# Sigmoid attention with a token mixer: one batch per partition half, row and column tiles throughout, whole-row q and k loads on one queue

## The chip, the cores and the metric

The kernel runs on one core of one Trainium2 chip (trn2). The metric is the time of one execution on the device in microseconds (us), inputs and outputs in the chip's main memory. Each kernel was run several times; each run carries a state, fast or slow, and only fast runs are compared. A profile is one execution; its span is 1.5 to 2.5 us shorter than the time of the same run.

In the profile lines PE is TensorE, PEld its weight loads, DVE VectorE, ACT ScalarE, POOL GpSimd; SPq and ACTq are the instruction queues of SyncE and ScalarE. A timeline line gives start and duration in us, engine, line of kernel.py, operation, output <- inputs, for TensorE the tile of the array (rows*columns) and the shape, and how many of them; in brackets stands how long the engine was idle before, and what ended that. On TensorE the outputs are ptq, ptk, px and pk (transposes of q, k, x and wk), sc (scores), pv (values), pw (wq/wk), pt (tmp = wk.T @ x), pm (mix) and po (output). The granted clock is the share of TensorE's full clock that it got in a stretch.

## The reference

```python
batch, n_heads, seq, head_dim = 8, 12, 448, 64
S = 448; scale = 1 / sqrt(64)
scores = scale * q @ k.T - log(S)
attn   = 1 / (1 + exp(-scores))             # sigmoid, no row sum
x      = (attn @ v)                          # 8 x 12 x 448 x 64 -> 8 x 448 x 768
# the token mixer, weights w_q, w_k (768 x 64), w_out (768 x 768)
wq, wk = x @ w_q, x @ w_k                    # 448 x 64 per batch
mixed  = (scale * wq @ wk.T) @ x             # the kernel computes wq @ (wk.T @ x)
out    = maximum(mixed, 0) @ w_out           # fp32, 8 x 448 x 768
```

Everything comes and goes in fp32: 11 MB each of q, k, v and output. On the chip it is cast to bf16. There is a sigmoid for each of 8 x 12 x 448 x 448 scores, and those are ScalarE's work.

## The kernel before

Work is cut into 4 units of two batches, and each unit into 6 pairs of heads. A pair is: loads, casts (GpSimd), transposes of q and k (TensorE, copied out by VectorE), 14 score matmuls, 7 sigmoids on two of them at a time (ScalarE), two bursts of values matmuls. The mixer of unit u-1 is dealt out among the scores of unit u by a list of estimated costs.

The loads alternate between two queues; `nc.scalar` is ScalarE's own instruction stream:

```python
queues = (nc.sync, nc.scalar)
def load_qk(u, j):
    for nm, src in (("q", q), ("k", k)):
        t = p_ld.tile([P, 2, NI * HD], F32, tag=nm + "32", name=nm + "32")
        for b2 in range(2):                              # 64 partitions each
            queues[b2].dma_start(out=t[64 * b2 : 64 * b2 + 64], in_=...)
# load_v: 4 transfers of 64 partitions, two on each queue; load_vr: 4 more per unit, in 256-byte pieces
```

Scores use the whole 128 x 128 array with zeros: the two heads of a pair lie on the two partition halves and kz holds each head's keys with zeros on the other half.

```python
for gg in range(NI):                                     # 7 groups of 2 score blocks
    sc = ps_s.tile([P, 2, 512], F32, ...)                # two buffers
    for slot in range(2):
        nc.tensor.matmul(sc[:, slot, 0:S], kzt[u, j][:, b2, m * P : (m + 1) * P], qt[u, j][:, b2, :], ...)
    nc.scalar.activation(at, sc[:, :, 0:S], ACTF.Sigmoid, bias=bias_t, scale=attn_scale)
    ...                                                  # values burst, then pieces of the mixer
```

Of the kernel before, what the change touches and what calls it, by code (L numbers as in the profile page):

```python
# [12 lines left out]
ALU = mybir.AluOpType  # L13

PV_COL = True
# [3 lines left out]
def kernel(  # L19
# [14 lines left out]

    nc = tc.nc
# [10 lines left out]
    KPOS = [2 * i if i < 4 else 2 * (i - 4) + 1 for i in range(NI)]  # L46
# [10 lines left out]
    p_vr = pool("vr", 2)  # L57
    p_w32 = pool("w32", 3)
    p_c16 = pool("c16", 2)
    p_qt = pool("qt", 2)  # L60
    p_at = pool("at", 10)
    p_x = pool("x", 2)
# [3 lines left out]
    ps_v = pool("ps_v", 1, space=bass.MemoryType.PSUM)  # L66
    ps_f = pool("ps_f", 3, space=bass.MemoryType.PSUM)


    NKZ = 3  # L70
    kz = [singles.tile([P, 2, NI * P], BF16, name=f"kz{n}") for n in range(NKZ)]
    if PV_COL:
        v16 = [[singles.tile([P, NJ, 2, 3, HD], BF16, name=f"v16{n}{b}") for b in range(2)] for n in range(2)]
        vr16 = [[singles.tile([P, NJ, P], BF16, name=f"vr16{n}{b}") for b in range(2)] for n in range(2)]
        vzero = [t for n in range(2) for t in vr16[n]]
    else:
        vz = [[singles.tile([P, NJ, NI, P], BF16, name=f"vz{n}{b}") for b in range(2)] for n in range(2)]
        vzero = [t for n in range(2) for t in vz[n]]
    wqbd = singles.tile([P, NI, 2, NP], BF16, name="wqbd")
    wkts = singles.tile([P, NI, 2, NP], BF16, name="wkts")  # L80
    wout16 = singles.tile([P, NC, D], BF16, name="wout16")
    wqk = [singles.tile([P, NC, P], BF16, name=f"wqk{b}") for b in range(2)]
    wq32 = singles.tile([P, NC, DH], F32, name="wq32")
    wk32 = singles.tile([P, NC, DH], F32, name="wk32")
    ident = singles.tile([P, P], F32)
    bias_t = singles.tile([P, 1], F32)
    ident16 = singles.tile([P, P], BF16)

    ctx.enter_context(tc.manual_schedule())


    queues = (nc.sync, nc.scalar)
    ld = {}

    def load_qk(u, j):
        for nm, src in (("q", q), ("k", k)):
            t = p_ld.tile([P, 2, NI * HD], F32, tag=nm + "32", name=nm + "32")
            for b2 in range(2):
                queues[b2].dma_start(  # L99
                    out=t[64 * b2 : 64 * b2 + 64],  # L100
                    in_=src[2 * u + b2, 2 * j : 2 * j + 2].rearrange("h (p i) d -> p h (i d)", i=NI),
                )
            ld[nm, u, j] = t

    def load_v(u, j):
        for b2 in range(2):
            t = p_ld.tile([P, 2, 3 * HD], F32, tag=f"v32{b2}", name="v32")
            base = v[2 * u + b2, 2 * j]

            for par, (off, step) in enumerate(((0, S + 4), (4, S - 3))):  # L110
                queues[par].dma_start(  # L111
                    out=t[64 * par : 64 * par + 64],
                    in_=bass.AP(
                        base.tensor, base.offset + off * HD,
                        [[NI * HD, NP], [step * HD, 2], [1, 3 * HD]],
                    ),
                )
            ld["v", u, j, b2] = t

    def load_vr(u):  # L120
        for b2 in range(2):
            t = p_vr.tile([P, NJ, HD], F32, tag=f"vr32{b2}", name="vr32")
            for hh, i in ((0, 3), (1, 0)):
                queues[hh].dma_start(
                    out=t[64 * hh : 64 * hh + 64],
                    in_=v[2 * u + b2].rearrange("(j h) (p i) d -> h i p j d", h=2, i=NI)[hh, i],
                )
            ld["vr", u, b2] = t


    def cast_qk(u, j, eng_q=nc.gpsimd):
        for nm, eng in (("q", eng_q), ("k", nc.gpsimd)):
            t16 = p_c16.tile([P, NI, 2, HD], BF16, tag=nm + "16", name=nm + "16")
            eng.tensor_copy(  # L134
                out=t16.rearrange("p i h d -> p h i d"),
                in_=ld.pop((nm, u, j)).rearrange("p h (i d) -> p h i d", i=NI),
            )
            ld[nm + "16", u, j] = t16

    def cast_v(u, j):  # L140
        for b2 in range(2):
            t = ld.pop(("v", u, j, b2))
            if PV_COL:
                nc.gpsimd.tensor_copy(  # L144
                    out=v16[u % 2][b2][:, j].rearrange("p h m d -> p (h m d)"),
                    in_=t.rearrange("p h x -> p (h x)"),
                )
            else:
                z = vz[u % 2][b2]
                for hh in range(2):  # L150
                    nc.gpsimd.tensor_copy(
                        out=z[:, j, 4 * hh : 4 * hh + 3, 64 * hh : 64 * hh + 64],
                        in_=t[:, hh].rearrange("p (m d) -> p m d", m=3),
                    )

    def cast_vr(u):
        for b2 in range(2):
            t = ld.pop(("vr", u, b2))
            for hh in range(2):
                r = slice(64 * hh, 64 * hh + 64)  # L160
                dst = vr16[u % 2][b2][r, :, r] if PV_COL else vz[u % 2][b2][r, :, 3, r]
                nc.gpsimd.tensor_copy(out=dst, in_=t[r])


    qt, kzt = {}, {}
    nkz = [0]

    def tr_q(u, j):
        st = {}

        def f(i):
            if i == 0:
                st["p"] = ps_f.tile([P, 2, NI, NP], BF16, tag="f", name="ptq")
            nc.tensor.transpose(  # L174
                st["p"][:, :, i, :], ld["q16", u, j][:, i].rearrange("p h d -> p (h d)"), ident16
            )
            if i == NI - 1:
                t = p_qt.tile([P, 2, NI * NP], BF16, tag="qt", name="qt")
                nc.vector.tensor_copy(out=t, in_=st["p"].rearrange("p b i n -> p b (i n)"))  # L179
                qt[u, j] = t  # L180
        return [(60, lambda i=i: f(i)) for i in range(NI)]

    def tr_k(u, j):
        st = {}

        def f(i):
            if i == 0:
                st["p"] = ps_f.tile([P, 2, NI, NP], BF16, tag="f", name="ptk")
            nc.tensor.transpose(  # L189
                st["p"][:, :, KPOS[i], :], ld["k16", u, j][:, i].rearrange("p h d -> p (h d)"), ident16  # L190
            )
            if i == NI - 1:
                z = kz[nkz[0] % NKZ]
                nkz[0] += 1
                for hh in range(2):
                    r = slice(64 * hh, 64 * hh + 64)
                    nc.vector.tensor_copy(  # L197
                        out=z[r, :, S * hh : S * hh + S],
                        in_=st["p"][r].rearrange("p b i n -> p b (i n)"),
                    )  # L200
                kzt[u, j] = z
        return [(60, lambda i=i: f(i)) for i in range(NI)]
# [4 lines left out]
    def mlp(u):  # L207
        xt = xts[u]
        st = {}

        def wqk_mm(b2, c):
            if c == 0:
                st["w", b2] = ps_f.tile([P, NI, NP], F32, tag="f", name="pw")
            nc.tensor.matmul(  # L214
                st["w", b2], wqk[b2][:, c, :], xt[c][:, :, b2, :],
                start=(c == 0), stop=(c == NC - 1),
            )
            if c == NC - 1:
                rq = slice(64 * b2, 64 * b2 + 64)
                rk = slice(64 - 64 * b2, 128 - 64 * b2)  # L220
                nc.vector.tensor_copy(out=wkts[rk, :, b2, :], in_=st["w", b2][rk])
                nc.vector.tensor_copy(out=wqbd[rq, :, b2, :], in_=st["w", b2][rq])  # L222

        def x_tr(i, c):
            if i == 0 and c == 0:
                st["xn"] = p_one.tile([P, NI, D], BF16, tag="xn", name="xn")
            if c == 0:
                st["px"] = ps_f.tile([P, D], BF16, tag="f", name="px")
            nc.tensor.transpose(  # L229
                st["px"][:, c * P : (c + 1) * P],  # L230
                xt[c][:, i].rearrange("p b n -> p (b n)"), ident16,
            )
            if c == NC - 1:
                nc.vector.tensor_copy(out=st["xn"][:, i, :], in_=st["px"])

        def wk_tr(i):
            if i == 0:
                st["pk"] = ps_f.tile([P, NI, 2, 64], BF16, tag="f", name="pk")
            nc.tensor.transpose(
                st["pk"][:, i].rearrange("p b n -> p (b n)"),  # L240
                wkts[:, i].rearrange("p b n -> p (b n)"), ident16,
            )
            if i == NI - 1:
                st["wkn"] = p_one.tile([P, NI, 2, 64], BF16, tag="wkn", name="wkn")
                for b2 in range(2):
# [245 lines left out]
```

## Time and profile before

| | before |
|---|---|
| time, median of 4 | 314.8 us (311.94 to 419.04; the 419 is a single slow run) |
| first sigmoid | 17.5 us |
| first unit, no mixer in it | 64.5 us |
| units 2, 3, 4 | 68, 69, 61 us |
| tail, from about the last sigmoid | 32.2 us |
| load rate from 2 to 42 us | 247 GB/s |

A unit is read from one wq/wk stage to the next. The first unit, which has neither mixer nor output in it, is hardly shorter than the others. No engine is full there.

### The profile page before, as it was taken

The numbers are of one execution on the slowest core, as the hardware profiler recorded it, in microseconds if no ns is written. First come the engines' busy times: TensorE is split into PE (matmuls) and PEld (weight loads), VectorE is DVE, ScalarE is ACT, GpSimd is POOL, SyncE is SP. The second block draws the span as 40 slices with busy tenths as digits, with TensorE's granted clock in tenths as the row PEclk, the third lists the DMA queues.
The fourth block names the chain that finished last, engine by engine and source line by source line (L and its number), as shares of the span: only waits on it lengthen the run. The fifth ranks groups of instructions, "written<-read, shape, count | busy, mean of one in ns | idle before, by whom it ended". The sixth has DMA issues, their size and how long they took to land.

```text
span 312.2 us, 4870 instructions
## 1 busy us (share of the span) xinstructions
PE 249.2 (80%) x1740; PEld 132.8 (43%) x1740; DVE 155.0 (50%) x271; ACT 175.6 (56%) x193; POOL 80.8 (26%) x128
## 2 busy tenths in 40 slices
PE   1476675777889889499869889599869889998994
PEld 0223222333445445255446445255445445545452
DVE  3522322333566746245646646245656646548662
ACT  0086375487656766467745766448745768770210
POOL 1640832553312302333032312323032303000000
PEclk9999859877999999799998999699999999999998
DMA  8999998656430365947990375948991265232076
GB/s 176 247 235 288 216 257 190 157 117 163 96 86 0 86 186 136 218 122 200 246 224 5 82 185 143 214 110 212 240 227 27 63 187 134 53 101 52 0 178 176
DMA packets 40984, 47.11 MB, mean 151 GB/s; under 512 B 12032, under 2 KB 36608, under 8 KB 40960
## 3 DMA queue, kind: packets, MB, share of 16 engines
q1 hardware_dynamic: 23936, 30.29, 39.8%
q10 hardware_dynamic: 17024, 16.52, 22.2%
q8 instruction: 13, 0.21, 0.3%
q14 instruction: 11, 0.09, 0.1%
HBM read 35.78 MB, written 11.01 MB: 150 GB/s over the span
## 4 chain that ended last, share of the span: by engine, by line
PE 50%; DMA 22%; ACTq 8%; ACT 6%; DVE 6%; issue 3%; POOL 2%; SPq 1%; POOLq 0%
PE sc L439 16%; PE po L281 15%; DMA q<-in_q_dram 10%; PE pv L368 8%; ACT at L446 6%; DMA k<-in_k_dram 5%; ACTq L99 4%; ACTq L111 3%; DMA vr<-in_v_dram 3%; PE pt L253 3%; DMA v<-in_v_dram 3%; PE ptk L189 2%; PE pm L265 2%; PE pw L214 2%; DVE kz L197 2%
## 5 line engine op out<-in xcount | busy, mean ns | idle before, releaser
L446 ACT ACTIVATE at<-sc,bias_t 128x896 bf16<-128x896 f32 x168 | 164.2, 1007 | 91.3 <-PE sc L439 38.2
L439 PE MATMUL sc<-qt,kz 128*128 128x448 bf16 x336 | 99.4, 383 | 41.2 <-ACT at L446 40.2
L281 PE MATMUL po<-wout,mx 128*128 128x384 bf16 x336 | 67.2, 335 | 0.0
L439 PEld LDWEIGHTS <-kz 128*128 128x128 bf16 x336 | 30.8, 102 | 74.4 <-issue 63.2
L134 POOL CAST q<-q 128x896 bf16<-128x896 f32 x23 | 21.5, 933 | 158.0 <-DMA q<-in_q_dram 113.5
L377 DVE CAST xt<-pv 128x448 bf16<-128x448 f32 x48 | 30.0, 625 | 48.5 <-PE pv L368 48.5
L287 DVE COPY o<-po 128x384 f32<-128x384 f32 x56 | 31.2, 558 | 36.2 <-PE po L281 35.7
L281 PEld LDWEIGHTS <-mx 128*128 128x128 bf16 x336 | 33.4, 100 | 26.0 <-issue 3.7
L197 DVE COPY kz<-ptk 64x896 bf16<-64x896 bf16 x48 | 29.8, 621 | 23.4 <-PE ptk L189 23.0
L368 PE MATMUL pv<-at,v 128*64 128x448 bf16 x288 | 39.1, 381 | 0.0
L179 DVE COPY qt<-ptq 128x896 bf16<-128x896 bf16 x24 | 15.0, 624 | 24.2 <-PE ptq L174 23.9
L134 POOL CAST k<-k 128x896 bf16<-128x896 f32 x24 | 22.4, 933 | 15.3 <-DMA k<-in_k_dram 10.2
L144 POOL CAST v<-v 128x384 bf16<-128x384 f32 x48 | 23.1, 506 | 5.9 <-DMA v<-in_v_dram 3.9
L368 PEld LDWEIGHTS <-v 128*64 128x64 bf16 x288 | 12.7, 113 | 24.3 <-issue 21.1
L272 ACT ACTIVATE mx<-pm 128x448 bf16<-128x448 f32 x24 | 13.0, 541 | 17.3 <-PE pm L265 17.3
L174 PE MATMUL ptq<-ident,q 128*128 128x128 bf16 x168 | 15.3, 228 | 9.2 <-DVE q L134 5.8
L189 PE MATMUL ptk<-ident,k 128*128 128x128 bf16 x168 | 19.3, 246 | 1.6 <-POOL k L134 1.6
L265 PE MATMUL pm<-wqbd,tmp 128*128 128x448 bf16 x48 | 15.6, 353 | 4.7 <-DVE kz L197 2.9
L174 PEld LDWEIGHTS <-q 128*128 128x128 bf16 x168 | 12.1, 102 | 14.9 <-DVE q L134 5.8
L189 PEld LDWEIGHTS <-k 128*128 128x128 bf16 x168 | 14.1, 111 | 9.2 <-issue 4.4
L368 PE MATMUL pv<-at,vr 128*64 128x448 bf16 x96 | 17.7, 362 | 0.0
L229 PE MATMUL px<-ident,xt 128*128 128x128 bf16 x168 | 14.5, 231 | 1.6 <-DVE wqbd L222 0.7
(35 smaller groups left out, 126.7 us busy)
## 6 DMA issues: line engine op xcount, KB each, us to landing
out_dram<-o SPq DMA_DIRECT2D x56, 192.0 KB, 2.7
q<-in_q_dram ACTq DMA_DIRECT2D x24, 224.0 KB, 3.6
q<-in_q_dram SPq DMA_DIRECT2D x24, 224.0 KB, 4.9
k<-in_k_dram ACTq DMA_DIRECT2D x24, 224.0 KB, 4.2
k<-in_k_dram SPq DMA_DIRECT2D x24, 224.0 KB, 5.5
v<-in_v_dram ACTq DMA_DIRECT2D x48, 96.0 KB, 4.7
v<-in_v_dram SPq DMA_DIRECT2D x48, 96.0 KB, 4.8
w<-in_moe_w_out_dram SPq DMA_DIRECT2D x6, 384.0 KB, 5.9
```

The lines of the kernel that those rows point to most:

```text
L134: eng.tensor_copy(out=t16.rearrange("p i h d -> p h i d"), in_=ld.pop((nm, u, j)).rearrange("p h (i d) -> p h i d", i=NI),)
L144: nc.gpsimd.tensor_copy(out=v16[u % 2][b2][:, j].rearrange("p h m d -> p (h m d)"), in_=t.rearrange("p h x -> p (h x)"),)
L174: nc.tensor.transpose(st["p"][:, :, i, :], ld["q16", u, j][:, i].rearrange("p h d -> p (h d)"), ident16)
L189: nc.tensor.transpose(st["p"][:, :, KPOS[i], :], ld["k16", u, j][:, i].rearrange("p h d -> p (h d)"), ident16)
L197: nc.vector.tensor_copy(out=z[r, :, S * hh : S * hh + S], in_=st["p"][r].rearrange("p b i n -> p b (i n)"),)
L265: nc.tensor.matmul(pm, st["tmp"][:, c * P : (c + 1) * P], wqbd.rearrange("p i b n -> p (i b n)")[:, hf * S : (hf + 1) * S], start=True, st ...
L281: nc.tensor.matmul(st["po"], st["mx"][c][:, i * P : (i + 1) * P], wout16[:, c, nb * NB : (nb + 1) * NB], start=(c == 0), stop=(c == NC - 1),)
L287: nc.vector.tensor_copy(out=st["o"][:, nb * NB : (nb + 1) * NB], in_=st["po"])
L368: nc.tensor.matmul(ps[c], w, ats[u, j, b2, 4 * hh + m if m < 3 else 3], start=(m == 0), stop=(m == 3),)
L377: nc.vector.tensor_copy(out=xts[u][j][:, :, b2, :], in_=ps)
L439: nc.tensor.matmul(sc[:, slot, 0:S], kzt[u, j][:, b2, m * P : (m + 1) * P], qt[u, j][:, b2, :], start=True, stop=True,)
L446: nc.scalar.activation(at, sc[:, :, 0:S], ACTF.Sigmoid, bias=bias_t, scale=attn_scale)
```

## The change

The intent: the two batches of a unit take the two partition halves. The transposes of a pair then write two column tiles (64 output rows each), the scores of a head are two row tiles (contraction 64 each, no zeros), and so on through the mixer. The loads of q and k become whole: 128 partitions (two heads x 64) per transfer, on SyncE's queue (one k at the start excepted); v stays in four transfers of 64 partitions. The mixer's parts come in blocks at fixed places. A one-element sigmoid at the start also brings ScalarE's table load forward: it took 1.28 us directly ahead of the first sigmoid before.

```diff
-    queues = (nc.sync, nc.scalar)
...
+    def load1(n, nm, eng):
+        t = p_ld.tile([P, 2, NI * HD], F32, ...)
+        eng.dma_start(out=t, in_=dict(q=q, k=k)[nm][2*u : 2*u+2, 2*j : 2*j+2].rearrange(
+            "b h (p i) d -> (h p) b (i d)", i=NI))
...
+    def scores(n, g):                       # 6 of these, plus one for the leftover keys in column tiles
+        h, m = divmod(g, 3)
+        for b2 in range(2):                 # HALF = partitions 0..63, 64..127
+            nc.tensor.matmul(sc[:, b2, 0:S], kts[n][HALF[b2], h, m*P : (m+1)*P], qts[n][HALF[b2], h, :], ...)
+        sigmoid(n, g, sc)
...
     for n, (u, j) in enumerate(pairs):
+        if n + 3 < N:                       # q, k three pairs ahead (were two)
+            load1(n + 3, "q", nc.sync)
+            load1(n + 3, "k", nc.sync)
+        if n + 2 < N:
+            load_v(n + 2, nc.sync)
...
+        if n + 1 < N: tr_q(n + 1)           # 14 column-tile transposes (were 7 whole ones)
+        scores_last(n)
+        if n + 1 < N: tr_k(n + 1)           # 16
+        if n >= 2: tr_x(n - 2)              # 16
+        if u > 0 and j == 1: mlp_wkn(u - 1)
+        scores(n, 0); scores(n, 1)
+        whole(left)                         # up to two output groups of 6 matmuls
+        scores(n, 2); scores(n, 3)
+        if n > 0: values(n - 1, 0); values(n - 1, 1)
+        if u > 0 and j == 1: mlp_tmp(u - 1)
+        scores(n, 4); scores(n, 5)
+        if u > 0 and j == 0: mlp_wqk(u - 1)
+        elif u > 0 and j == 1:
+            for c in range(NC): mlp_mix(u - 1, c)
+            outs += outs_of(u - 1)
+        else: whole(left - 1)
```

(The one-line `if` forms are shortened here.)

## The prediction

> **What bounds the kernel now.** I read the busy shares and the chain of the page first, then the stages by windows (cut at the first sigmoid, just ahead of the wq/wk matmuls of each unit of two batches, and at the last values matmuls), then who waits for whom on ScalarE, then two stretches of the timeline.
>
> ```profile
> PE 249.2 (80%) x1740; PEld 132.8 (43%) x1740; DVE 155.0 (50%) x271; ACT 175.6 (56%) x193; POOL 80.8 (26%) x128
> ...
> PE 50%; DMA 22%; ACTq 8%; ACT 6%; DVE 6%; issue 3%; POOL 2%; SPq 1%; POOLq 0%
> ...
> L446 ACT ACTIVATE at<-sc,bias_t 128x896 bf16<-128x896 f32 x168 | 164.2, 1007 | 91.3 <-PE sc L439 38.2
> ```
>
> TensorE is busiest, but it has only half of the chain; 30% of the chain are transfers and the issuing of transfers on ScalarE's queue. The stages say where:
>
> ```profile
> 0.00:17.50 17.50, 5.09 (x31) 3.16 (x32) 7.99 (x15) 1.30 (x2) 7.34 (x18) 1.00 0.90 216
> 17.50:82.00 64.50, 46.00 (x264) 20.67 (x264) 18.71 (x30) 40.88 (x43) 25.17 (x38) 0.84 0.82 197
> 82.00:150.00 68.00, 58.27 (x435) 31.74 (x435) 36.72 (x64) 43.35 (x49) 18.57 (x28) 0.97 0.52 129
> 150.00:219.00 69.00, 58.93 (x423) 32.80 (x423) 36.98 (x65) 43.11 (x48) 18.67 (x28) 0.93 0.65 155
> 219.00:280.00 61.00, 54.96 (x412) 29.48 (x409) 34.92 (x61) 43.27 (x48) 11.08 (x16) 1.00 0.55 132
> 280.00:312.20 32.20, 26.00 (x180) 15.01 (x179) 19.66 (x37) 3.69 (x7) 0.00 (x0) 0.96 0.39 98
> ```
>
> Columns: stretch, length, busy us of PE, PEld, DVE, ACT, POOL, then granted clock, DMA share, GB/s. A start of 17.5 us without a sigmoid; a first unit with nothing of the mixer in it that is almost as long (64.5) as the units with it (68, 69, 61); a tail of 32.2. The first unit is not bound by an engine: it holds 46.0 us of PE and 40.9 of ACT. The reason is in ScalarE's order:
>
> ```profile
> ACT at L446 <- PE sc L439: 38.2, 75, 1.9
> ACT at L446 <- DMA q<-in_q_dram: 29.6, 11, 5.6
> ACT L446 <- DMA q<-in_q_dram: 16.2, 1, 16.2
> ```
>
> ```profile
> 121.79 0.60 ACTq L99 DMA_DIRECT2D q<-in_q_dram  x1
> 122.51 0.60 ACTq L99 DMA_DIRECT2D k<-in_k_dram  x1
> 123.15 1.34 ACTq L124 DMA_DIRECT2D vr<-in_v_dram  x2
> 125.36 2.85 ACTq L111 DMA_DIRECT2D v<-in_v_dram  x2
> 128.31 1.01 ACT L446 ACTIVATE at<-sc,bias_t 128x896 bf16<-128x896 f32 x1 [5.59 <-DMA q<-in_q_dram]
> ```
>
> Four to six load issues of 0.60 us stand in front of each pair's sigmoids, in order. The built order shows that each issue also waits for an earlier transfer, because all loads share eight completion semaphores. Here the sigmoid stood still for 5.6 us and TensorE, which has two score buffers, behind it. Where no such wait falls, TensorE is dense:
>
> ```profile
> 236.18 0.54 PE L439 MATMUL sc<-qt,kz 128*128 128x448 bf16 x2
> 236.56 1.30 PE L253 MATMUL pt<-xn,wkn 128*128 128x384 bf16 x7
> 237.70 0.54 PE L439 MATMUL sc<-qt,kz 128*128 128x448 bf16 x2
> 238.17 0.76 PE L368 MATMUL pv<-at,v 128*64 128x448 bf16 x6
> 238.76 0.36 PE L368 MATMUL pv<-at,vr 128*64 128x448 bf16 x2
> 239.05 0.55 PE L439 MATMUL sc<-qt,kz 128*128 128x448 bf16 x2
> ```
>
> From start to start: two scores 0.38 us (0.19 each), seven tmp matmuls of 384 columns 1.14 (0.163 each), a values burst of eight column-tile matmuls 0.88, so the two tiles do run together (0.10 a piece, not 0.19). Before the burst the scores took 0.47 instead of 0.38: about 0.1 us for the change of tiling; the change back, inside the 0.88, costs about the same. In a quiet stretch seven 128x128 transposes took 0.39 us, 0.055 each.
>
> **What the Trainium skill says.** "TensorEngine Tiling (Array Packing)", Key Properties: tiles work independently, changing the tiling mode drains TensorE; the 0.09 us above agrees in kind. "TensorE: Matmul & The Clock Gate", Part 3: row tiles run concurrently, 3.07x measured for four; no row tile is in this trace. "ScalarE: Activation LUTs", What ACT_TABLE_LOAD costs: an ACTIVATE with a pointer bias takes about 280 + 0.833 N ns and neighbours overlap by about 93 ns; for N = 896 that is 1026, the trace has 1007, and pairs of sigmoids take 1.91 us, so 0.90 from start to start. "DMA: Bandwidth & Descriptors", Rules for kernel authors: two transfers to partition halves share the same engines, use one of 128 partitions. Unproved here; but the first windows move 216 to 241 GB/s with two queues full, which looks like a ceiling near 250.
>
> **The change part by part.**
> *Loads.* One q and one k transfer per pair instead of four, all on SyncE's queue (one k excepted), q and k three pairs ahead instead of two; the separate vr loads in 256-byte pieces go. Bytes stay near 47 MB (wq and wk are read twice, +0.4). ScalarE loses about 104 issues of 0.6 us, 62 us of its sequencer, and all waits for transfers. At 245 GB/s the traffic is 192 us: not the bound over the whole span, but just in time in the first unit. Up to k of pair 6, needed in its last segment, 10.3 MB must land: 42 us plus 2 of latency.
>
> *Scores.* Per pair 12 row-tile matmuls (6 times at 0.19 if two run together) and 4 column-tile ones for the leftover 64 keys (2 times at 0.19): 1.52 us instead of 14 x 0.19 = 2.66. *Values* stay 8 pairs of matmuls, 1.52 us. *wq/wk* stay 24 half matmuls for 12 whole ones. *mix* 12 matmuls in pairs, *tmp* 8 pairs for 14.
>
> *Transposes* go the other way: q 14, k 16, x 16 per pair of heads, each 64 columns wide, for 7 + 7 + 7. At a perfect pairing they would cost 0.028 us each, with none 0.055; **I choose 0.04**, because each keeps its own weight load. Per pair of heads 46 x 0.04 = 1.84 us against 21 x 0.055 = 1.16.
>
> TensorE per unit with mixer (six pairs), us:
> - before: scores 84 x 0.19 = 16.0; values 12 x 0.98 (with both changes of mode) = 11.8; transposes 133 x 0.055 = 7.3; wq/wk 2.3; tmp 14 x 0.163 = 2.3; mix 12 x 0.19 = 2.3; out 84 x 0.163 = 13.7; sum 55.7, in units that took 61 to 69.
> - after: scores 9.1; values 9.1; transposes 292 x 0.04 = 11.7; wq/wk 2.3; tmp 1.3; mix 1.1; out 13.7; seven or so changes of mode per pair, 45 x 0.1 = 4.5; sum 52.8.
>
> So TensorE itself gains only about 3 us per unit. ScalarE needs 42 x 0.90 + 6 x 0.5 = 41 us. Outputs and values now stand in bursts of 1.5 to 2 us between scores, with two score buffers of 0.9 us each, and the six mix steps end on a relu or a VectorE pass of 0.62 us each; I add 3 us per unit: **56**.
>
> First unit: no mixer, TensorE 6 x 5.6 (1.84 + 1.52 + 1.52 + 0.7) = 34, ScalarE 38, loads until about 44 to 55 on the clock: **44** us of length instead of 64.5. Start: q lands near 5.2 as now, its cast 0.63, 14 and 16 cold transposes near 0.1 each, two copies, then the next pair's q transposes stand before the first scores: first sigmoid near **11** instead of 17.5. Tail: two values groups, wq/wk, wkn, tmp, six mix steps (3.7) and then all 14 output groups x 0.98 = 13.7 and a last transfer of 2.7: **30** instead of 32.2.
>
> VectorE falls a little: kt in one copy for two, wq/wk in two for four. GpSimd casts 3 us per pair. Neither bounds.
>
> Sum: 11 + 44 + 3 x 56 + 30 = 253 us of span; the timed runs are 1.5 above the span now: **254 us**.
>
> **The rivals.** (a) *Tiled transposes do not pair, or their weight loads show*: 0.06 us and more each makes 292 x 0.02 = 6 us per unit, about 20 in all: 272. For it: more than twice as many. Against: weight loads ran fully hidden before. (b) *Row tiles do not overlap*: 6 x 6 x 0.19 = 6.8 us per unit for scores plus 2.3 + 1.1: some 30 us in the three units, 284. Against: the skill's measurement. (c) *Transfers become the bound*: one queue with eight transfers in flight, outputs that wait for VectorE ahead of loads. At 200 GB/s the span could not go under 235, and the first unit would be 10 to 15 longer: 265. For it: 0.82 DMA share already. Against: two to three pairs of lead. (d) *Transposes pair fully and coupling is nil*: 52.8 - 3.5 = 49 per unit: about 238.
>
> **Range and chances.** 254, from 232 (d and a faster start) to 280 (a and c together). To miss 2% two rivals would have to come true in full: faster 0.93, same 0.05, slower 0.02.
>
> **What would show it.** ScalarE's waits for loads (29.6 + 16.2) should vanish and its queue's share of the chain go to zero; the first sigmoid near 11; first unit 44; units 54 to 58 with PE near 90% busy; scores starting 4 to 30 ns apart in pairs; transposes near 0.04 from start to start. I am wrong if transposes need 0.06 or more, if paired scores start 0.19 apart, if the sigmoid still waits for transfers after the first unit, or if units stay above 60.

## The result, and the profile after

The changed kernel takes 250.75 us (median of 4, 250.45 to 251.0), the kernel before 314.8. The ratio is 0.7989, with a 95% interval of 0.7925 to 0.8053. Ratios here are the mean time of one kernel's fast runs over that of the other's of the same rounds, so not quite the ratio of the medians quoted. Executions over 1.5% slower than the fastest of the same kernel are left out of the means.

Busy shares and the chain that ended last, from the page of the changed kernel:

```profile
PE 215.9 (87%) x2480; PEld 116.7 (47%) x2480; DVE 132.2 (53%) x230; ACT 171.7 (69%) x194; POOL 75.5 (30%) x84
...
PE 72%; ACT 17%; issue 5%; DVE 2%; DMA 2%; ACTq 0%
```

Transfers and ScalarE's issuing had 30% of the chain and have 2%. TensorE goes from half of it to 72%.

The stages of the changed kernel, cut at the first sigmoid, at the first scores of each unit, and just before the last sigmoid; columns as in the prediction (stretch, length, busy us of PE, PEld, DVE, ACT, POOL, granted clock, DMA share, GB/s):

```profile
0.00:9.70 9.70, 3.66 (x52) 2.61 (x54) 3.76 (x13) 1.60 (x3) 3.65 (x9) 1.00 0.83 255
9.70:52.10 42.40, 31.55 (x418) 16.92 (x417) 16.35 (x26) 38.29 (x42) 25.10 (x27) 0.96 1.09 295
52.10:108.10 56.00, 51.48 (x610) 27.87 (x611) 30.74 (x53) 42.93 (x49) 17.93 (x20) 0.97 0.69 185
108.10:163.00 54.90, 52.36 (x628) 28.02 (x624) 32.57 (x56) 42.62 (x49) 17.13 (x18) 1.00 0.74 202
163.00:218.40 55.40, 52.96 (x594) 27.96 (x588) 32.16 (x55) 42.24 (x49) 11.68 (x12) 1.00 0.57 144
218.40:248.50 30.10, 23.94 (x201) 13.32 (x200) 16.61 (x30) 4.05 (x7) 0.00 (x0) 0.96 0.41 105
```

Read it against the table of before: start 17.5 to 9.7, first unit 64.5 to 42.4, the three units 198 to 166.3, tail 32.2 to 30.1. The two tables are cut at different marks; by one mark for both, the first sigmoid of each unit, the units were 64.2, 68.0, 70.7 and 60.0 us and are 43.1, 55.9, 54.9 and 55.6. The first unit is now ScalarE's (38.3 of 42.4 us busy), the others TensorE's (52.4 of 54.9).

Who ScalarE waits for in the changed kernel (waiter, line, what it waited for: us in all, times, longest):

```profile
ACT at L169 <- PE sc L177: 23.7, 19, 6.8
ACT at L169 <- PE sc L187: 23.7, 35, 2.0
```

No line with a transfer is left in that list; before there were 29.6 and 16.2 us for q alone.

One stretch of TensorE in the changed kernel, fully warm:

```profile
107.67 0.58 PE L139 MATMUL ptq<-ident,q 128*64 128x128 bf16 x14
108.09 0.55 PE L177 MATMUL sc<-qt,kt 128*64 128x448 bf16 x4
108.47 0.55 PE L155 MATMUL ptk<-ident,k 128*64 128x128 bf16 x13
...
108.92 0.39 PE L223 MATMUL px<-ident,xt 128*64 128x128 bf16 x7
...
109.46 0.70 PE L187 MATMUL sc<-qt,kt 64*128 64x448 bf16 x4
110.09 1.15 PE L289 MATMUL po<-wout,mx 128*128 128x384 bf16 x6
```

From start to start: 14 q transposes 0.42 us (0.030 each), 4 scores in column tiles 0.38 (two at a time), 16 k transposes 0.45 (0.028). The 16 x transposes take 0.54 up to the first row-tile scores; a change of tiling is in that, and without 0.1 for it they are 0.028 each too.

### The profile page after: what moved, and what is told of

It is laid out like the page before. It is cut to its first block, busy times and chain, and to the rows that moved or that the text cites. A ratio compares the mean times of both kernels' runs of the same rounds, so it can differ in the third digit from the quotient of the medians.

```text
span 248.5 us, 6124 instructions
## 1 busy us (share of the span) xinstructions
PE 215.9 (87%) x2480; PEld 116.7 (47%) x2480; DVE 132.2 (53%) x230; ACT 171.7 (69%) x194; POOL 75.5 (30%) x84
## 4 chain that ended last, share of the span: by engine, by line
PE 72%; ACT 17%; issue 5%; DVE 2%; DMA 2%; ACTq 0%
PE po L289 19%; PE pv L203 16%; ACT at L169 15%; PE sc L187 12%; PE ptk L155 5%; PE ptq L139 5%; PE sc L177 5%; PE px L223 4%; PE pw L236 4%; ACT mx L280 2%; PE pt L263 2%; DMA q<-in_q_dram 2%; PE pm L275 1%; DVE tmp L268 1%; PE pk L251 1%
## 5 line engine op out<-in xcount | busy, mean ns | idle before, releaser
L169 ACT ACTIVATE at<-sc,bias_t 128x896 bf16<-128x896 f32 x168 | 158.8, 1006 | 49.3 <-PE sc L177 23.7
L187 PE MATMUL sc<-qt,kt 64*128 64x448 bf16 x288 | 47.2, 358 | 14.4 <-ACT at L169 14.0
L125 POOL CAST v<-v 128x1024 bf16<-128x1024 f32 x24 | 25.0, 1040 | 38.4 <-PE pv L203 21.0
L187 PEld LDWEIGHTS <-kt 64*128 64x128 bf16 x288 | 12.3, 93 | 43.3 <-issue 40.8
L203 PEld LDWEIGHTS <-v 128*64 128x64 bf16 x384 | 19.7, 109 | 17.0 <-issue 6.1
L159 DVE COPY kt<-ptk 128x1024 bf16<-128x1024 bf16 x24 | 16.6, 690 | 9.7 <-PE ptk L155 9.7
L139 PE MATMUL ptq<-ident,q 128*64 128x128 bf16 x336 | 15.5, 238 | 6.0 <-DVE q L116 6.0
L155 PEld LDWEIGHTS <-k 128*64 128x64 bf16 x336 | 15.1, 120 | 4.2 <-issue 0.8
L224 DVE COPY xn<-px 128x1024 bf16<-128x1024 bf16 x24 | 16.4, 681 | 0.4 <-PE px L223 0.4
L177 PE MATMUL sc<-qt,kt 128*64 128x448 bf16 x96 | 14.5, 382 | 2.2 <-ACT at L169 2.2
L155 PE MATMUL ptk<-ident,k 128*64 128x128 bf16 x336 | 16.4, 233 | 0.0
L279 DVE TENSOR_SCALAR mx<-pm 128x448 bf16<-128x448 f32 x24 | 13.8, 619 | 2.6 <-PE pm L275 2.4
```

The costliest lines, as they stand in the source:

```text
L125: nc.gpsimd.tensor_copy(out=t.rearrange("p b h s d -> p (b h s d)"), in_=v32[n % NV].rearrange("p b h s d -> p (b h s d)"),)
L139: nc.tensor.transpose(ps[HALF[b2], i].rearrange("p h n -> p (h n)"), t16[:, b2, i, :], ident16)
L155: nc.tensor.transpose(ps[HALF[b2], pos].rearrange("p h n -> p (h n)"), src, ident16)
L177: nc.tensor.matmul(sc[HALF[b2], h, 0:S], kts[n][:, h, 3 * P + 64 * b2 : 3 * P + 64 * b2 + 64], qts[n][:, h, :], start=True, stop=True,)
L187: nc.tensor.matmul(sc[:, b2, 0:S], kts[n][HALF[b2], h, m * P : (m + 1) * P], qts[n][HALF[b2], h, :], start=True, stop=True,)
L203: nc.tensor.matmul(ps[HALF[b2]], v16s[n][:, b2, h, slot, :], rhs, start=(m == 0), stop=(m == 3))
```

## The experiments

Eleven kernels were run. My theory Q was that most of the gain comes from ScalarE no longer standing still at load issues. Its rivals were T (TensorE's tiling carries the gain) and D (it is the longer lead of the loads).

### One word of the kernel before

```diff
-    queues = (nc.sync, nc.scalar)
+    queues = (nc.sync, nc.sync)
```

> The kernel before with one word changed: all loads on SyncE's queue, none on ScalarE's. Theory Q (most of the 64 us come from ScalarE no longer standing still at load issues): 265 to 285 us, ScalarE waits for transfers near 0, first unit 45 to 52 us instead of 64.5. Rival T (the tiling of TensorE's work carries the gain): above 300 us. Rival D (the lead of the loads matters, not the queue): above 300 here too, and only the run with one more pair of lead falls.

Measured: 269.48 us (268.63 to 271.05). The stages of this run:

```profile
0.00:12.20 12.20, 2.78 (x16) 1.46 (x16) 5.49 (x10) 1.31 (x2) 4.59 (x14) 1.00 0.79 180
12.20:62.00 49.80, 38.20 (x277) 18.16 (x279) 20.60 (x35) 40.57 (x44) 28.61 (x42) 1.00 1.01 248
62.00:121.00 59.00, 56.08 (x435) 30.70 (x429) 37.18 (x65) 44.33 (x48) 18.81 (x28) 1.00 0.70 176
...
238.00:268.20 30.20, 23.96 (x168) 14.11 (x165) 18.49 (x35) 3.26 (x6) 0.00 (x0) 0.98 0.41 104
```

Of the 63.7 us between the spans of the two profiles (312.2 and 248.5), this word alone brings 44. In its own rounds it is 40 us between the means of the fast runs (309.9 and 269.7) and 45 between the medians. T falls as the main cause, and so does D in its first half. The first unit goes from 64.5 to 49.8, a mixer unit to 59. In that unit TensorE is busy 56.1 us: this is what its work of before costs when nothing disturbs it, close to the 55.7 that the prediction had added up. (In these rounds only two of seven runs of the kernel before, 308.17 and 311.67 us, count as fast. The ratio is 0.8701, 0.8589 to 0.8813; the record's verdict is "unclear" for all four experiments of these rounds. Their ratios have a lower base than those of the other experiments.)

The clock changed with the word, and no run separates the two. The mean granted clock was 0.942 to 0.963 in the seven runs of the kernel before and 0.998 to 0.999 in the four here; in the first unit it was 0.84 and is 1.00. Among the runs of the kernel before, those at 0.942 to 0.945 took over 314 us and the one at 0.963 308.17. So part of the 40 to 45 us may have come through the clock; whether the low clock followed from the waits is not shown. A rough estimate for the first unit: in the run with batches below, 10.3 us at half the clock went with a first unit 1.7 us longer than that of the changed kernel; the 0.84 before stands for 20 us at half the clock, so some 3 us of the 18 that this unit loses here (64.2 to 46.2 us by its sigmoids).

### The same, with one more pair of lead

```diff
+    p_ld = pool("ld", 4)                       # was 3
+    load_qk(0, 2); load_v(0, 2)                # at the start
-        if n + 2 < len(pairs):
+        if n + 3 < len(pairs):                 # loads of pair n + 3
```

> As the one-queue run, with q, k and v loaded three pairs ahead instead of two (load pool of 4). Theory Q: within 5 us of the one-queue run. Rival D: 20 us or more below it. Either way what then separates it from the changed kernel (250.75) is the share of TensorE's work and order.

Measured: 271.12 us (fast runs 270.64 to 271.32). Nothing gained: D falls for this kernel; in the changed kernel the lead was not varied.

### The changed kernel with loads put back on ScalarE's queue

```diff
-            load1(n + 3, "k", nc.sync)
+            load1(n + 3, "k", nc.scalar)       # also at the start
-                eng.dma_start(out=t[HALF[par], ...
+                (nc.sync, nc.scalar)[par].dma_start(out=t[HALF[par], ...     # half of v
```

> The changed kernel with the k loads and half of the v loads put back on ScalarE's queue: about 70 issues of 0.5 to 0.6 us ahead of sigmoids. Theory Q: 270 to 290 us, sigmoids that wait for transfers come back with 15 us or more in total, first unit above 52 us. Rival T: at most 257 us. Rival D: at most 257, as the lead stays three pairs.

Measured: 270.06 us (269.62 to 271.41), 19 us more; it only just reaches the range. Who ScalarE waits for here, the lines with loads:

```profile
ACT at L169 <- DMA v<-in_v_dram: 10.2, 1, 10.2
...
ACT at L169 <- DMA q<-in_q_dram: 5.3, 1, 5.3
ACT at L169 <- POOL v L125: 3.8, 1, 3.8
```

Waits for loads are back, 15.5 us by name, and 3.8 for a cast whose buffer a load needs. But the 10.2 end at the very first sigmoid, at 13.6 us, which in the changed kernel comes at 9.7: only 3.9 of them are new. The loss falls on the start (3.9 us) and the first unit (56.2 us by its sigmoids, where the changed kernel has 43.1); the units with mixer take 55.6, 56.4 and 56.5 (55.9, 54.9, 55.6). So the lead of three pairs, kept, does not shield ScalarE in the first unit, where a load issue in its stream holds up the sigmoids behind it; later the three issues per pair cost little here. In the kernel before, four to six stood ahead of each pair. The clock is again a part that is not separated: 0.88 in this first unit, 0.96 in that of the changed kernel.

### What gives the higher load rate: two splits

The prediction took 245 to 250 GB/s for a ceiling; the changed kernel loads at 295. Two kernels split each q and k load into two transfers of 224 KB, once by partition half and once by batch:

```diff
+        for h2 in range(2):     # a_halves: 64 partitions, both batches
+            eng.dma_start(out=t[HALF[h2]], in_=...[2*u : 2*u+2, 2*j + h2].rearrange("b (p i) d -> p b (i d)", i=NI))
```
```diff
+        for b2 in range(2):     # a_batches: 128 partitions, one batch
+            eng.dma_start(out=t[:, b2], in_=...[2*u + b2, 2*j : 2*j+2].rearrange("h (p i) d -> (h p) (i d)", i=NI))
```

> The changed kernel with each q and k load split into two transfers of 64 partitions on the same queue. The changed kernel moved 294 GB/s in its first unit, before it was about 245. If the width of 128 rows gives that rate, it falls below 260 GB/s here and the time rises by 3 to 15 us. If one queue or the missing 256-byte pieces give it, it stays near 290 and the time within 2 us.

> The changed kernel with each q and k load split by batch instead of by partition half: two transfers of 224 KB that still reach 128 partitions, on the same queue. It separates what the run with halves left open, where the rate of the first 40 us fell from 295 to 243 GB/s. If the number of bytes that eight transfers hold in flight sets the rate, it stays near 245 and the time near 257. If the rows of 128 partitions set it (or the issue, which took SyncE 0.63 us for a half and 0.47 for twice the bytes in 128 rows), the rate is back near 290 and the time at 250 to 253.

Halves: 257.46 us (254.5 to 258.85; the highest is slow, the three fast runs have a mean of 256.5). Batches: 251.66 (250.95 to 252.58). The window of 2 to 42 us, in the order changed kernel, halves, batches:

```profile
2.00:42.00 40.00, 27.30 (x356) 15.33 (x358) 14.46 (x25) 30.37 (x34) 21.18 (x22) 0.96 1.08 295
```
```profile
2.00:42.00 40.00, 25.99 (x330) 14.72 (x332) 13.71 (x23) 27.73 (x31) 17.70 (x18) 1.00 1.05 243
```
```profile
2.00:42.00 40.00, 28.28 (x348) 15.48 (x349) 14.46 (x25) 29.01 (x32) 20.50 (x21) 0.87 1.03 292
```

The last column is GB/s. The number and the size of the transfers are the same in both splits; only the 64 partitions bring the rate of the kernel before back. So the 128 rows raise the rate, not the single queue: the run with two queues and whole rows moved 311 GB/s from 2 to 22 us, the changed kernel 309, the kernel before 244. Two things go with 128 rows and are not separated here: how the rows spread, and the issue itself, which took SyncE 0.63 us for a half of 224 KB and 0.47 us for a whole of 448 KB. The issue is a real rival: the issue records of SyncE fill 34.4 of the 40 us above with halves, 32.7 with batches and 29.3 in the changed kernel. In time the rate is worth 5 to 7 us. In the profile of the halves, the fastest of its runs, 3.0 of the 4.2 us lie in the start (first sigmoid at 12.7 instead of 9.7 us); the first unit takes 43.6 us instead of 43.1.

### Do the row tiles overlap?

```diff
-                sc[:, b2, 0:S], kts[n][HALF[b2], h, ...], qts[n][HALF[b2], h, :],
+                sc[:, b2, 0:S], kts[n][HALF[0], h, ...], qts[n][HALF[0], h, :],
```

The second batch's scores are wrong. (The check against the reference passed all the same: with these inputs the sigmoid hardly depends on the scores. A passing check proves little about this part.)

> The changed kernel with both score matmuls of a pair taken from partitions 0 to 63 (the second batch's scores are wrong on purpose), so that the two cannot lie in different row tiles. Theory: row tiles overlap, and each of the 6 pairs of scores per pair of heads costs 0.19 us more of TensorE, 1.14 in all: 18 pairs with mixer x 1.14 = 20 us and 0 to 5 in the first unit, so 268 to 278 us. Rival: the two did not overlap to begin with (or TensorE has slack): within 3 us of 250.75.

Measured: 275.56 us (median; fast runs 271.95 and 274.49, the other two and the profile slow), ratio to before 0.8703. Against the changed kernel's 0.7989 that is 9% or 22 us more. A row tile here is half of the array's rows. One group of four scores in this run:

```profile
116.59 0.93 PE L187 MATMUL sc<-qt,kt 64*128 64x448 bf16 x4
```

The four take 0.93 us where the changed kernel's take 0.55 (its line of 68.34 us further below): here each starts 0.19 to 0.20 us after the one before, there the two of a pair start 0.002 to 0.006 us apart. So the row tiles do overlap. The 22 us are near the sum, but not all of them are its work: in the profile, a slow run, the three units with mixer are 15 us longer together, for which the sum gave 20, and the first unit is 10.8 us longer at a granted clock of 0.78 (0.96 in the changed kernel).

### Do the column-tile transposes overlap?

```diff
-        for i in range(NI):
-            for b2 in range(2):
+        for b2 in range(2):          # all of one half, then all of the other; tr_k and tr_x alike
+            for i in range(NI):
```

> The changed kernel with its column-tile transposes in another order, all of one half and then all of the other, result unchanged. Theory: neighbours in different halves overlap, 0.028 to 0.034 us each; in one half they cost 0.055: 46 x 0.024 = 1.1 us per pair of heads, 18 x 1.1 = 20 and some in the first unit: 266 to 276 us. Rival: the rate comes from the narrow weight loads, not from overlap: within 3 us of 250.75.

Measured: 256.86 us (255.58 to 257.89): 6 us more, neither the 20 nor the 3. The timeline shows why. In the program every ptk transpose stands before every px; in this run of it:

```profile
37.54 0.58 PE L155 MATMUL ptk<-ident,k 128*64 128x128 bf16 x10
...
37.96 0.28 PE L155 MATMUL ptk<-ident,k 128*64 128x128 bf16 x2
38.02 0.24 PE L223 MATMUL px<-ident,xt 128*64 128x128 bf16 x1
38.07 0.22 PE L155 MATMUL ptk<-ident,k 128*64 128x128 bf16 x1
38.10 0.22 PE L223 MATMUL px<-ident,xt 128*64 128x128 bf16 x1
```

The first px transposes (lower half) start before the last ptk ones (upper half). So an order of blocks undoes only part of the overlap: a column tile can start work that stands some places further on in the program. My expectation had missed this, and the 6 us are not the price of overlap as a whole. But the records of this run settle the rival that the rate comes from the narrow weight loads. Four ptk transposes of one half, before the other half joins in (the same timeline, cut at 37.72 us):

```profile
37.54 0.39 PE L155 MATMUL ptk<-ident,k 128*64 128x128 bf16 x4
```

One lasts 0.22 us, so the four start 0.055 us apart, like the whole-array ones. In the changed kernel two of them, one in each half, start 0.003 us apart, and a new pair every 0.056: the 0.028 us are two tiles at a time, not a cheaper transpose.

### Bursts: the values split, and everything split

The prediction added 3 us per unit for TensorE's bursts outrunning two score buffers. In the first unit of the changed kernel a pair takes 7.21 us where seven sigmoids need about 6.4. First only the values:

```diff
         scores(n, 2)
+        if n > 0: values(n - 1, 0)
         scores(n, 3)
-        if n > 0: values(n - 1, 0); values(n - 1, 1)
+        if n > 0: values(n - 1, 1)
```

> The changed kernel with the two values groups on two sides of one scores step instead of back to back. Theory: in the first unit a pair takes 7.21 us where ScalarE needs 6.4, because 1.63 us of values outrun two score buffers; split, a pair takes 6.4 to 6.6: 4 to 5 us less there, 1 to 3 less in the rest: 242 to 247 us. Rival: the 7.21 are TensorE's own changes of mode and work, one more change per pair: 251 to 254 us.

Measured: 249.63 us (248.53 to 250.73), ratio 0.794. The intervals overlap with the changed kernel's: unclear, about 1 us by the medians. Four of the first unit's pairs did fall, from 7.21 to 6.73 us, which would be 2.8 us over six. In this profile the unit as a whole gained nothing (43.2 us for 43.4): its second pair took 9.22 us instead of 7.34, in a stretch in which the granted clock was 0.50 (15 to 20 us) and 0.64 (20 to 25 us).

Then everything: one block at most between two scores steps, three output groups per pair, wq/wk and mix in two parts. The order of a pair after the second of a unit, condensed:

```diff
+        scores_last(n); tr_q(n + 1); tr_k(n + 1); scores(n, 0); tr_x(n - 2); scores(n, 1); values(n - 1, 0)
+        scores(n, 2); values(n - 1, 1); scores(n, 3); whole(); scores(n, 4); whole(); scores(n, 5); whole()
```

> The changed kernel with TensorE's other work laid between the scores steps as evenly as it goes: values split, at most one output group at a time, three output groups per pair instead of four and two, wq/wk and mix in two parts, the next pair's q and k transposes together. Theory (the 3 us per unit that I added for bursts are real, and more like 5): first unit 39, units 51 to 53: 232 to 240 us. Rival (TensorE's work itself is the bound of the units, 53 to 55 us each with its changes of mode): 244 to 250 us.

Measured: 252.03 us (251.92 to 252.51), ratio 0.8031: not better, and the theory falls (the time lies above the rival's 244 to 250 too). TensorE in a mixer unit of this kernel:

```profile
141.26 0.36 PE L187 MATMUL sc<-qt,kt 64*128 64x448 bf16 x2
141.56 1.15 PE L295 MATMUL po<-wout,mx 128*128 128x384 bf16 x6
142.64 0.36 PE L187 MATMUL sc<-qt,kt 64*128 64x448 bf16 x2
142.93 1.15 PE L295 MATMUL po<-wout,mx 128*128 128x384 bf16 x6
```

In these lines TensorE does not wait at all, and the kernel is no faster. A pair of scores takes 0.30 us between two other tilings, where two pairs in a row take 0.38 (0.19 each); an output group takes 1.08, where in the tail, without a change, it takes 0.97. So each change of tiling costs 0.10 us. This kernel has 13 of them in such a pair, the changed kernel 7. What the even order takes away in waits it seems to pay in changes: six more per pair at 0.10 us.

### Where the waits really were: the mix block

With the pairs' scores as marks, the six pairs of a mixer unit of the changed kernel take 8.86, 12.76, 9.86, 9.25, 7.65 and 7.64 us. The second stands out. Its end, TensorE in the changed kernel:

```profile
68.34 0.55 PE L187 MATMUL sc<-qt,kt 64*128 64x448 bf16 x4
68.73 0.68 PE L275 MATMUL pm<-wqk,tmp 64*128 64x448 bf16 x4
69.79 0.35 PE L275 MATMUL pm<-wqk,tmp 64*128 64x448 bf16 x1 [0.39 <-DVE mx L279]
70.32 0.35 PE L275 MATMUL pm<-wqk,tmp 64*128 64x448 bf16 x1 [0.18 <-DVE mx L279]
71.19 1.82 PE L275 MATMUL pm<-wqk,tmp 64*128 64x448 bf16 x6 [0.53 <-ACT mx L280]
72.95 0.96 PE L139 MATMUL ptq<-ident,q 128*64 128x128 bf16 x14
```

Twelve mix matmuls, 1.1 us of work, take from 68.73 to 72.95. Each step needs a relu on ScalarE, and the relus stand behind the two sigmoids of the scores just issued. In this unit part of the stretch ran at a lower clock; in the next unit, at full clock, the block takes nearly as long (124.72 to 128.78) and the second pair 12.25 us. The mix steps use the same row tiling as the scores, so they can lie beside scores of the next pair without a change of tiling:

```diff
+        if u > 0 and j == 2: mlp_mix(u - 1, 2); mlp_mix(u - 1, 3)     # after scores 0, 1
+        if u > 0 and j == 2: mlp_mix(u - 1, 4); mlp_mix(u - 1, 5)     # after scores 2, 3; then outs
-            for c in range(NC): mlp_mix(u - 1, c)
+            mlp_mix(u - 1, 0); mlp_mix(u - 1, 1)
```

> The changed kernel with the six mix steps no longer in one block at the end of the second pair of a unit: two there, two and two beside scores of the next pair (the same tiling, so no change of mode). Theory: in the changed kernel that pair takes 13 us where its TensorE work is under 10, as the relus stand behind two sigmoids on ScalarE; spread, each of the three units loses about 3 us: 240 to 244 us. Rival: the time comes back in the pairs that take the mix steps and the outputs over: 248 to 251.

Measured: 248.11 us (247.55 to 248.92), ratio 0.7923 (0.7878 to 0.7968): about 2.6 us less, though its interval still overlaps with the changed kernel's. By the same marks the second pair falls from 12.76 to 9.25 us and the unit from 56.02 to 54.24: half of the 3.5 us came back, most of it in the fifth pair (7.65 to 9.25), which now holds four output groups instead of two. In the next unit, at full clock in both, the second pair falls by 2.9 us and the unit only from 54.88 to 54.28. The rival was nearer the truth than the theory.

With the values split in the first unit only, the outputs dealt 2, 4, 3, 3, 1, 1 and the very first scores ahead of the next transposes:

> As the run with mix spread, and in the first unit the values groups on two sides of a scores step (2.8 us, read from the split run), outputs 2, 4, 3, 3, 1, 1 per pair, and the first scores of all ahead of the next pair's transposes. Changes of mode stay at about seven per pair. Theory: 236 to 241 us. Rival (TensorE's work is all there is): 247 to 251.

Measured: 246.1 us (244.86 to 247.46), ratio 0.7858 (0.7811 to 0.7905). The interval lies clear of the changed kernel's (0.7925 to 0.8053): 1.6% less (0.7858 / 0.7989), the best of all, and short of the 236 to 241 expected; the rival had said 247 to 251. Its first unit takes 41.1 us and its mixer units 53.5 to 54.5, of which TensorE is busy 49 to 52.

## Why the prediction was right or wrong

The time was 250.75 us for 254 predicted. The main mechanism was right; part of the agreement in the sum is luck. Point by point:

- **Loads leave ScalarE's queue: right, and the largest part.** Moving them in the kernel before gives 44 of 63.7 us, with the clock in it; putting some back gives up 19 us. The other 19.7 us, from the one-queue kernel to the changed one, are tiling, order, whole rows and the earlier table load together. ScalarE's waits for loads went to none, and its queue's share of the chain to 0%.
- **Start: 9.7 us for 11.** The cold transposes were put at 0.1 us each; the first 14 took 0.79 us, 0.056 each.
- **First unit: 42.4 us for 44, from a wrong rate.** The ceiling of 245 to 250 GB/s was the mis-sized term: whole rows moved at 295. But "just in time" was no bad guess: at the 243 GB/s of the halves this unit is hardly longer (43.6 us for 43.1 by its sigmoids), and the start is 3 us later.
- **Transposes: mis-sized.** I chose 0.04 us; they took 0.028 to 0.030. That is 292 x 0.011, about 3 us per unit less, the case of rival (d).
- **Row tiles: right.** The scores start 0.002 to 0.006 us apart in pairs, and 22 us more go when the two of a pair cannot overlap; rival (b) had said 30, with wq/wk and mix.
- **Changes of mode: right.** 0.1 us, about seven per pair.
- **Bursts: the term of 3 us per unit was too small, and its reason partly wrong.** With the transposes at their true cost, TensorE's sum is 52.8 - 3 = 50 us against units of 54.9 to 56.0, so 5 to 6 us stand beside it. By the stage table TensorE is idle for 4.5, 2.5 and 2.4 of them; the rest is work and changes that the sum had too low, and no run says which. The largest wait found is the mix block behind two sigmoids, about 4 us for 1.1 us of matmuls, which the prediction named only in passing; splitting the bursts in general gained nothing.
- **Units 56.0, 54.9, 55.4 for 56, tail 30.1 for 30.** The units agree because the two errors, 3 us too much for transposes and about 3 too little for the rest, cancel. The 56 is a right number with two wrong terms: luck.

The rivals: (a) and (c) did not come; (d) came true in its first half only. Its 238 does not follow from the prediction's own terms: 11 + 44 + 3 x 49.3 + 30, and 1.5 above the span, are 234. What stays open is how much of the 40 to 45 us came through the clock, and how much of the 128-row gain is the spread of rows and how much the shorter issue.

## What to carry to other kernels

Keep transfers out of the instruction stream of an engine that is needed all the time: each issue, and whatever it waits for, holds up the work behind it; here one word was worth 40 to 45 us of some 310. Load across all 128 partitions (5 to 7 us here). Once TensorE is the bound, count its changes of tiling (0.1 us each) before you interleave more finely, and place a step that ends on another engine where that engine's queue is short.

## What the Trainium skill lacked or had wrong

- "TensorEngine Tiling (Array Packing)", Key Properties, says that a change of tiling mode drains TensorE, without a cost. Here it is 0.10 us: 1.08 us against 0.97 for an output group of six matmuls with and without a change.
- "TensorE: Matmul & The Clock Gate", Part 3, says that matmuls start and end in program order. In the run with reordered transposes, a lower-half px transpose started at 38.02 us, ahead of the upper-half ptk transpose at 38.07, which stands before it in the program. Such a step stands 63 times in that run's trace, and never in the changed kernel's. The starts of two column tiles are not in program order; the ends in the profile are modelled and tell nothing.
- The same page, Part 4, gives about 275 ns for a 128 x 128 transpose in a kernel and no spacing in a stream of them. The profile's durations here are 0.22 to 0.25 us, but in a stream they follow each other at 0.055 us whole and at 0.028 to 0.030 us in column tiles; for a sum it is this spacing that counts.
- "DMA: Bandwidth & Descriptors", Rules for kernel authors, advises against splitting by partition halves and gives no size. Here 243 GB/s against 295 whole, and 292 when split by batch.
- The same page, Issuing engines are not separate DMA queues, says that issuing from several engines only saves the issue time. It lacks the cost on the other side: about 0.6 us per load issue, and the waits in front of it, in ScalarE's own stream cost 40 to 45 us here, the clock included.
